# Attention and a gated feed-forward block on one core: when the loads of batch 2 and of the later queries are issued, a new planned order, and who turns tile 4

## The chip, the cores and the metric

One core of a Trainium2 chip. The time is the device time of one launch in microseconds (us). The engines are named as the profile names them: PE is TensorE (PEld its weight loads), DVE is VectorE, ACT is ScalarE, POOL is GpSimd, SP is the sync engine, which here only issues DMAs.

## The reference

```python
def _attn_ref(q, k, v):                     # 8 batches, 8 heads, 576 positions, 64 wide
    theta = np.pi / 2.0 * pos / S
    def phi(x, c, s):
        r = np.maximum(x, 0.0)
        return np.concatenate([r * c, r * s], axis=-1)
    q_p, k_p = phi(q, cos_w, sin_w), phi(k, cos_w, sin_w)
    kv = np.einsum('bhsf,bhsd->bhfd', k_p, v)
    z = np.sum(k_p, axis=2)
    num = np.einsum('bhsf,bhfd->bhsd', q_p, kv)
    den = np.einsum('bhsf,bhf->bhs', q_p, z)[..., None] + 1e-06
    return num / den

def _moe_ref(x, w_gate, w_val, w_out):      # x: 4608 tokens x 512; 1536 hidden
    g = x @ w_gate
    silu = g * (1.0 / (1.0 + np.exp(-g)))
    return silu * (x @ w_val) @ w_out
```

All inputs and the output are float32 in memory; the kernel casts its loads to 16 bits on the way in.

## The kernel before, in words

**Tiles and groups.** The 4608 tokens are 36 tiles of 128 rows (a batch is four and a half of them), and four tiles make one of nine groups (`tg` 0 to 8). For each batch `b` the kernel loads keys, values and queries (`load`, `load_turned`, on POOL's DMA queue: a key or value load is one instruction, a query load two), weighs them (relu on ACT, `vmul` on DVE), multiplies keys by values on PE (`kv_job`, the line L706), and turns the weighed queries by one long DMA on SP's queue (`phit<-r_q`, L905). For each tile `tile_jobs` (L823) then multiplies the turned queries with the key-value product, divides, and leaves a 128x512 tile `x`. The next stage needs that tile transposed (`xT`): `turn_job` does it by a DMA on SP's queue (L737), or, where its argument `by_pe` is true, by four transposes on PE and a copy on ACT (L745 and L597).

**The feed-forward part.** Group 0 and group 1 are computed plainly (L430, L928): gate and value products of 128x512 tiles. From group 2 on, gates are computed with a seven-product scheme (`block_jobs`, L999: each product is four matmuls of 256 columns), which first needs sums and differences of the turned tiles (`x_sum_jobs`, L972 on DVE, out of all four tiles of the group). The set `VAL` says for which groups the value products use that scheme as well, from `VAL_FROM` on; elsewhere `plain_val` computes them plainly. The scheme's summed weights are made once on DVE, by `weight_sums`. `out_jobs` (L1162) is the last product of a group, and `store_jobs` writes its rows.

**What sets the order.** From line 570 on nothing is issued at once: every piece is a `Job` with a duration for each engine that may do it and a list of jobs that it comes after, and `order_once` lays all of them out by a list schedule: at each step, for the engine that is free first, the most urgent ready job. What comes out is the program's order on each engine, fixed before the run; on the chip each instruction waits for its inputs. The planner starts its clock where the hand-written first part (`words`) ends; the first planned matmul of the profile stands at 27.5 us. `LOADED` gives the landing times of the loads of that first part, on the planner's clock. A DMA of the plan is put behind one running mark:

```python
            if j.dma:
                moved[0] = max(t + j.dma[0], moved[0]) + j.dma[1]
                j.done = moved[0] + LATER
```

with (1900, 600) ns for an `xT` transposition, (2500, 3300) for a load, and `LATER` 1500; due times count `X_LAND` 5200 for `xT`. `SEEDS` shake the urgencies, one number for each 10 us of PE's plan.

**Loads that are held.** `batch_loads` puts a tiny POOL copy (`hold_job`, L859) ahead of some loads, which reads a tile that must have landed first, so that the loads start only then. Everything behind that copy on POOL's queue, the stores among it, waits with it. Before the change: batch 2's keys and values wait for `xT` of tile 4; batch 3's queries for batch 2's turned queries; 3's keys and values for `xT` of tile 10; 4's queries, keys and values for 3's turned queries; 5's queries for `xT` of tile 15; 5's keys and values and 6's queries for 4's turned queries; 6's keys and values and 7's queries for 5's; 7's keys and values for 6's.

Of the kernel before, what the change touches and what calls it, by code (L numbers as in the profile page):

```python
# [19 lines left out]
def kernel(  # L20
# [584 lines left out]
    def relu_on(eng, out, in_):  # L605
# [7 lines left out]
    S_POOL = (1, 2, 4)  # L613
    S_GROUPS = ()
    LOADED = {("k", 1): 0.0, ("v0", 1): 6910.0, ("v1", 1): 8410.0, ("q0", 0): 2840.0, ("q0", 1): 10600.0, ("q1", 1): 18800.0,
              ("q", 2): 21600.0}
    WO_AT = ((0, 2, 11850.0), (2, 4, 13100.0), (4, 8, 15600.0), (8, 12, 18100.0))
    W_AT = {8: (1080.0, 2390.0), 10: (4150.0, 5460.0)}

    wg4 = wg_sb.rearrange("p (k c) (u w x) -> p w k c u x", k=2, w=2, x=P)  # L620
    wv4 = wv_sb.rearrange("p (k c) (u w x) -> p w k c u x", k=2, w=2, x=P)
# [112 lines left out]
    def turn_job(t, x, after, by_pe=False, key=None):  # L734
        if not by_pe:
            def fn(j):
                nc.sync.dma_start_transpose(out=xT_of(t), in_=one(x_all, x))  # L737
            J_["xT", t] = Job({"SP": 1450}, fn, after=after + J_.get(("xT_read", t // OUT - 3), []), put=[x], tail=X_LAND, dma=(1900.0, 600.0))
            return
        r = Room("bank")  # L740

        def fn(j):
            ps = bank(r).bitcast(FP16).rearrange("p (k x) -> p k x", x=P)
            for kc in range(KC):
                nc.tensor.transpose(out=ps[:, kc], in_=one(x_all, x)[:, kc * P:(kc + 1) * P], identity=ident16)  # L745
        mm = pe(230, fn, key, after=after, get=[r], put=[x])

        def fn(j):
            copied(j.eng, xT_of(t), bank(r).bitcast(FP16).rearrange("p (k x) -> p k x", x=P)[:, 0:KC])
        J_["xT", t] = Job({"ACT": sc(512)}, fn, after=[mm], put=[r])  # L750

    X_LAND = 5200.0
    PHI_LAND = 11500.0

    def half_tile_jobs(t, key, after, by_pe=False):
# [96 lines left out]
    def load_job(b, nm, after, lands, behind):  # L852
        def fn(j):
            (load_turned if nm == "q" else load)(b, nm)
        J_["load", b, nm] = Job({"POOL": 1600 if nm == "q" else 780}, fn, after=after, tail=lands, behind=behind, dma=(2500.0, 3300.0))

    def hold_job(read, after):
        def fn(j):
# [3 lines left out]
        return jb  # L862

    def batch_jobs(b, key):
        loaded_q = [J_["load", b, "q"]] if b > 2 else []
        landed = 0.0 if loaded_q else LOADED["q", 2]
        phis = []
        before = J_.get(("turned", b - 1), []) if b > 2 else J_["qt1"]

        def home():  # L870
            if (b, "q") not in st:
                st[b, "q"] = rel.tile([P, G, NC, 2, D], BF16, name="r_q")
            return st[b, "q"]
        if b in PHI_ACT:
            for c in range(NC):
                for w in range(2):
                    def fn(j, c=c, w=w):
                        nc.scalar.activation(out=home()[:, :, c, w], in_=raws[b, "q"][:, :, c], func=AF.Relu,
                                             scale=tanq[:, c:c + 1] if w else 1.0)
                    phis.append(Job({"ACT": 412}, fn, after=loaded_q + before + J_["tanq"], rel=landed))  # L880
        elif b in PHI_SWAP:
            for g in range(0, G, 2):
                def fn(j, g=g):
                    relu_on(j.eng, home()[:, g:g + 2, :, 0], raws[b, "q"][:, g:g + 2])
                phis.append(Job({"DVE": d4(1152)}, fn, after=loaded_q + before, rel=landed))
            for c in range(NC):
                def fn(j, c=c):
                    nc.scalar.activation(out=home()[:, :, c, 1], in_=raws[b, "q"][:, :, c], func=AF.Relu,  # L888
                                         scale=tanq[:, c:c + 1])
                phis.append(Job({"ACT": 430}, fn, after=loaded_q + before + J_["tanq"], rel=landed))  # L890
            J_["q_read", b] = list(phis)
        else:
            for g in range(G):
                def fn(j, g=g):
                    relu_on(j.eng, home()[:, g, :, 0], raws[b, "q"][:, g])
                re_ = Job(RELU_Q, fn, after=loaded_q + before, rel=landed)
                J_.setdefault(("q_read", b), []).append(re_)

                def fn(j, g=g):
                    tt(out=home()[:, g, :, 1], in0=home()[:, g, :, 0], in1=tabq2, op=ALU.mult)  # L900
                phis += [re_, Job({"DVE": d2(576)}, fn, after=[re_] + J_["tabq"])]
        J_["phi", b] = phis
        def fn(j):
            phit[b] = phip.tile([P, G, NC, SH, 2], BF16, name="phit")
            nc.sync.dma_start_transpose(out=phit[b].rearrange("p g c s e -> p (g c) (s e)"),  # L905
                                        in_=st[b, "q"].rearrange("p g c w d -> p (g c w d)"))
        turned = [Job({"SP": 7500}, fn, after=phis + J_.get(("tiles", b - 2), []), tail=PHI_LAND - 7500, dma=(2800.0, 6400.0))]
        J_["turned", b] = turned
        done = []
        for g in range(G):  # L910
            def fn(j, g=g):
                relu_on(j.eng, raws[b, "k"][:, g], raws[b, "k"][:, g])
            done.append(Job(RELU_K, fn, after=[J_["load", b, "k"]]))
            done.append(weight_job(b, g, [J_["load", b, "v"]] + ([J_["kvmm", b - 1]] if b > 2 else [])))
        J_["weighed", b] = done
        kv_job(b, key, done)

# [420 lines left out]
    for jj in range(J):  # L1338
        mm, o = turn_q_jobs(1, jj, 0, CUT, (0, 12.0 / 16), [rs[jj]])
        qa.append(o)  # L1340
        qmm.append(mm)
    plain_out_jobs((0, 0.76, 0.015))
    HALF_AT = (12.2, 12.6, 13.2, 13.8)
    for t, s, p in zip(range(4, 8), HALF_AT, (0, 1, 1, 1)):
        half_tile_jobs(t, (0, s / 16), lambda jj: [qa[jj]] + J_["qt0"] + J_["kv", 1], bool(p))
    for jj in range(J):
        mm, o = turn_q_jobs(1, jj, CUT, NC, (0, 15.5 / 16), [rs2])
# [41 lines left out]
    P2_AT = 3  # L1389
    P3_AT = {**{k_: 1.0 for k_ in range(1, 7)}, 7: 3.1}  # L1390
    GATE = set(range(2, NTG))
    VAL_FROM = 2
    VAL = {(tg, u) for tg in range(VAL_FROM, NTG) for u in range(3)}

    PLAIN = "g1 g3p v0 g7 g6 v2 g2 v1 g5 v3 g4".split()
    LAST = "v1 g3p v7 v6 v2 - v5 v4 - v3".split()
# [28 lines left out]

    APART = range(9, B)
    LAND = (6500.0, 7500.0, 8500.0)
    batch_loads(lambda: xT[1][0:1, 0, 0, 0:2], [J_["xT", 4]], [(2, "k"), (2, "v")])
    batch_jobs(2, (1, KV_AT[2] / 4))
    for tg in range(1, NTG):  # L1430
        b = tg + 2
        tiles = list(zip(range(max(9, 4 * tg + 4), 4 * tg + 8), TILES.get(tg + 1, ())))
        if 2 < b < B:
            def phit_read(b=b):
                return phit[b - 1][0:1, 0, 0, 0]
            names = {3: [(3, "q")], 4: [(4, "q"), (4, "k"), (4, "v")], 5: [(5, "k"), (5, "v"), (6, "q")],
                     6: [(6, "k"), (6, "v"), (7, "q")], 7: [(7, "k"), (7, "v")]}[b]
            batch_loads(phit_read, J_["turned", b - 1], names)
        for t, s in tiles:
            tile_jobs(t, (tg, s / 4))  # L1440
            if t == 10:
                batch_loads(lambda: xT[2][0:1, 2, 0, 0:2], [J_["xT", 10]], [(3, "k"), (3, "v")])
            if t == 15:
                batch_loads(lambda: xT[3][0:1, 3, 0, 0:2], [J_["xT", 15]], [(5, "q")])
        if b < B:
            batch_jobs(b, (tg + 1, KV_AT[b] / 4))
        if tg not in GATE:
            for fc in range(FC):
                plain_fc(tg, fc, (tg, fc / 4))
        else:  # L1450
            x_sum_jobs(tg)
            if ("wsum", "G") not in J_:
                weight_sums("G", wg4, {n: [J_["kvmm", 1]] for n in (2, 3, 4)}, list(gate_reads))
            if ("wsum", "V") not in J_ and (tg, 0) in VAL:
                weight_sums("V", wv4, {2: [J_["kvmm", 1]], 3: J_["num_done"], 4: J_["num_done"]}, list(val_reads))
            for u in range(3):
                at = places(tg, u)
                rooms, silus = silu_jobs(tg, u, block_jobs(tg, u, "G", gate_order(tg, u)))
                if (tg, u) in VAL:
                    order = [at[f"v{n}"] for n in (1, 7, 6, 2, 5, 4, 3)]  # L1460
                    block_mul_jobs(tg, u, rooms, silus, block_jobs(tg, u, "V", order))
                else:
                    for n, (i, w) in enumerate(((0, 0), (0, 1), (1, 0), (1, 1))):
                        plain_val(tg, u, i, w, rooms, silus, at[f"v{n}"])
# [24 lines left out]
    def order_once(nominal, seeds):  # L1489
# [31 lines left out]
            j.start = j.done = j.eng = None  # L1521
        free = {k: [(0.0, n) for n in range(n_)] for k, n_ in SIZE.items()}
        free["bank"] = [(t, n) for t, n in zip(BANK_AT, sorted(range(8), key=lambda x: used[x]))]
        is_filled, moved = [False] * 8, [LOADED["q", 2]]
        users = {}
        missing = {j: len(j.after) + len(j.behind) for j in jobs}
        est0 = {}
# [120 lines left out]
        return max(j.done for j in jobs if "PE" in j.engs)  # L1648

    RESERVE = 1  # L1650
    LATER = 1500.0
    SEEDS = (13881, 22536, 22536, 22536, 0, 12166, 85132, 39172, 44287, 22698, 22698, 53394, 50335, 50335, 92939, 92939, 92939, 0, 83505, 94269, 84613, 0, 0, 25880, 25880, 20639, 0)
    SHAKE = 1500.0
    WINDOW = 10000.0
    PACK = True
# [40 lines left out]
```

## Time and profile before

| | |
|---|---|
| median of three runs | 307.04 us (305.6; 307.04; and one of 1069.84) |
| the profiled execution's own time | 309.23 us |
| its span, first to last instruction | 307.4 us |
| mean granted clock of PE | 0.986 |
| PE busy | 295.6 us, 96% |
| DVE, ACT, POOL busy | 249.9, 201.0 and 70.3 us |
| read from memory, written to it | 37.75 MB, 9.44 MB |

The profiled execution took 2.19 us more than the median, and 1.83 us of its time lie outside the span. The page shows each engine's busy share in 40 slices of 7.7 us; below it stand the DMA engines' share and the clock that PE was granted. The other views used here are the waits by engine, the chain of work that ended last, the timeline of one engine, busy times by stretches, and the DMA issues of a stretch with the time to their landing.

### The profile page before, as it was taken

To read this page: it belongs to the slowest core of one execution; us is meant where nothing else is said; L and a number is where in the kernel's file an instruction comes from. 1 tells how busy PE (TensorE), PEld (TensorE's weight loads), DVE (VectorE), ACT (ScalarE), POOL (GpSimd) and SP (SyncE) were. 2 spreads that over 40 slices of the span, in tenths; PEclk is the share of its full clock that TensorE was granted. 3 is DMA by queue.
4 is the path that set the end of the run, shared out by engine and by line. 5 is a ranking of instruction groups with operands and counts; after the bars stand their busy time and mean duration, and the time that the engine had idled before them with its cause. 6 is when DMAs were issued, how large, how long until landed. Compare 5 with 4: busy or idle time off the path is not lost.

```text
span 307.4 us, 7913 instructions
## 1 busy us (share of the span) xinstructions
PE 295.6 (96%) x3170; PEld 237.2 (77%) x3170; DVE 249.9 (81%) x507; ACT 201.0 (65%) x427; POOL 70.3 (23%) x126
## 2 busy tenths in 40 slices
PE   8999999999999999995999999999999999999991
PEld 4597455455887988883888889888888988888880
DVE  7766769999978998893798994999779959967971
ACT  8564448954897795993589659986475556636430
POOL 7754402010208021800323202200220050002020
PEclk9999999999999999997899999999999999999998
DMA  7999999997899999999499792670262153002026
GB/s 259 225 197 197 205 204 140 224 147 125 125 203 186 193 161 151 141 187 232 60 211 186 156 171 71 120 145 13 57 109 46 19 124 67 0 2 68 2 70 138
DMA packets 72357, 41.02 MB, mean 133 GB/s; under 512 B 49280, under 2 KB 69248, under 8 KB 72320
## 3 DMA queue, kind: packets, MB, share of 16 engines
q0 software_dynamic: 24992, 24.91, 49.2%
q1 hardware_dynamic: 46880, 15.21, 27.4%
q10 hardware_dynamic: 448, 0.39, 0.6%
q8 instruction: 25, 0.41, 0.5%
q14 instruction: 12, 0.10, 0.1%
HBM read 37.75 MB, written 9.44 MB: 153 GB/s over the span
## 4 chain that ended last, share of the span: by engine, by line
PE 87%; DMA 7%; ACT 1%; DVE 1%; SPq 1%; issue 1%; DVEq 0%; ACTq 0%
PE banks L999 39%; PE banks L1162 24%; PE banks L928 10%; DMA xT<-x 4%; PE banks L430 3%; PE banks L1271 3%; PE banks L706 3%; DMA ht<-in_k_dram 2%; PE banks L823 2%; SPq L151 1%; PE banks L364 1%; PE banks L766 1%; ACT sg L1058 1%; PE banks L1305 0%; ACT banks L597 0%
## 5 line engine op out<-in xcount | busy, mean ns | idle before, releaser
L1131 POOL DMA_DIRECT2D out_dram<-ob x56 | 29.6, 537 | 125.0 <-ACT ob L599 91.6
L1092 DVE TENSOR_TENSOR ht<-sg,banks 128x512 f16<-128x512 bf16 x63 | 42.3, 682 | 3.2 <-PE banks L999 3.1
L1162 PEld LDWEIGHTS <-ht 128*128 128x128 f16 x384 | 37.8, 98 | 5.4 <-issue 0.5
L1058 ACT ACTIVATE sg<-banks 128x512 bf16<-128x512 f32 x63 | 35.8, 597 | 7.2 <-PE banks L999 5.9
L597 ACT COPY banks<-banks 128x512 f32<-128x512 f32 (+1 forms) x51 | 29.4, 581 | 15.4 <-PE banks L1162 9.4
L999 PEld LDWEIGHTS <-wgs_sb 128*128 128x128 f16 x336 | 32.7, 99 | 8.5 <-DVE kvt L972 3.6
L1019 DVE TENSOR_TENSOR banks<-m,banks 128x512 f32<-128x512 f32 x42 | 28.9, 692 | 9.1 <-PE banks L999 6.2
L999 PEld LDWEIGHTS <-wg_sb 128*128 128x128 f16 x336 | 32.6, 98 | 4.0
L999 PE MATMUL banks<-kvt,wgs_sb 128*128 128x256 f16 x216 | 32.3, 278 | 3.5 <-DVE kvt L972 3.4
L999 PEld LDWEIGHTS <-wv_sb 128*128 128x128 f16 x336 | 32.3, 98 | 4.3 <-issue 0.2
L599 ACT ACTIVATE ob<-banks 128x512 f32<-128x512 f32 x34 | 20.0, 597 | 23.6 <-PE banks L1162 18.7
L1162 PEld LDWEIGHTS <-sums 128*128 128x128 f16 x288 | 28.2, 99 | 3.6
L597 ACT COPY m<-banks 128x512 f32<-128x512 f32 x42 | 24.4, 588 | 8.1 <-PE banks L999 8.1
L1162 PE MATMUL banks<-wo_sb,ht 128*128 128x256 f16 x192 | 26.3, 276 | 0.2 <-ACT banks L597 0.2
L999 PE MATMUL banks<-xT,wg_sb 128*128 128x256 f16 x168 | 25.7, 276 | 0.0
L1162 PE MATMUL banks<-wt_sb,sums 128*128 128x256 f16 x192 | 25.4, 279 | 0.0
L999 PE MATMUL banks<-xT,wv_sb 128*128 128x256 f16 x168 | 24.8, 273 | 0.0
L1162 PE MATMUL banks<-wt_sb,ht 128*128 128x256 f16 x192 | 22.4, 272 | 0.0
L1058 ACT ACTIVATE sg<-m 128x512 bf16<-128x512 f32 x21 | 13.2, 631 | 10.8 <-DVE m L1027 10.7
L269 DVE TENSOR_TENSOR v<-raw_kv,tab 128x1152 bf16<-128x1152 bf16 x27 | 19.3, 754 | 0.4 <-ACT raw_kv L451 0.4
L888 ACT ACTIVATE r_q<-raw_q,tanq 128x256 bf16<-128x256 bf16 x45 | 19.6, 502 | 0.0
L999 PE MATMUL banks<-kvt,wv_sb 128*128 128x256 f16 x144 | 19.5, 273 | 0.0
(153 smaller groups left out, 566.6 us busy)
## 6 DMA issues: line engine op xcount, KB each, us to landing
out_dram<-ob POOLq DMA_DIRECT2D x56, 128.0 KB, 2.9
raw_kv<-in_k_dram POOLq DMA_DIRECT2D x7, 576.0 KB, 7.7
raw_q<-in_q_dram POOLq DMA_DIRECT2D x12, 288.0 KB, 8.3
raw_kv<-in_v_dram POOLq DMA_DIRECT2D x6, 576.0 KB, 9.3
out_dram<-ob SPq DMA_DIRECT2D x12, 128.0 KB, 2.6
wg_sb<-in_moe_w_gate_dram POOLq DMA_DIRECT2D x5, 256.0 KB, 9.1
wv_sb<-in_moe_w_val_dram POOLq DMA_DIRECT2D x5, 256.0 KB, 9.5
wo_sb<-in_v_dram SPq DMA_DIRECT2D x2, 576.0 KB, 4.1
```

The source lines that it names most:

```text
L269: nc.vector.tensor_tensor(out=v2s[b == 1][:, g, :, :, 0:D], in0=(first if b == 0 and g == 0 else {"v": raw_of(b, "v")})["v"][:, g].unsquee ...
L430: nc.tensor.matmul(out=st["f", tg, fc, lo][i], lhsT=(wg_sb, wv_sb)[i][:, kc, fs], rhs=xT[tg][:, ts, kc], start=(kc == 0), stop=(kc == KC - 1))
L597: nc.scalar.copy(out=out, in_=in_)
L599: nc.scalar.mul(out=out, in_=in_, mul=mul)
L888: nc.scalar.activation(out=home()[:, :, c, 1], in_=raws[b, "q"][:, :, c], func=AF.Relu, scale=tanq[:, c:c + 1])
L928: nc.tensor.matmul(out=bank(r), lhsT=w[:, kc, fc * P:(fc + 1) * P], rhs=xT[tg][:, :, kc], start=(kc == 0), stop=(kc == KC - 1))
L999: nc.tensor.matmul(out=to[:, i], lhsT=a[:, c, 2 * u + i], rhs=x()[:, :, c], start=first and i == 0 and c == 0, stop=c == KH - 1, skip_grou ...
L1019: tt(out=bank(c), in0=one(m7_all, m).rearrange("p i x -> p (i x)"), in1=bank(b), op=ALU.add)
L1058: nc.scalar.activation(out=gates(rooms[w])[:, :, jh * HT:(jh + 1) * HT], in_=src, func=AF.Silu, scale=DOWN)
L1092: tt(out=ht[:, 4 * u + w:4 * u + w + 3:2, jh * HT:(jh + 1) * HT], in0=gates(rooms[w])[:, :, jh * HT:(jh + 1) * HT], in1=src.rearrange("p ( ...
L1131: {"POOL": nc.gpsimd, "SP": nc.sync, "ACT": nc.scalar}[j.eng].dma_start(out=out_v[idx // NC, idx % NC][:, cols], in_=ob_of(t)[e * SH:(e + ...
L1162: nc.tensor.matmul(out=to, lhsT=a[:, kc, i * P:(i + 1) * P], rhs=b[:, kc], start=first and kc == 0 and i == 0, stop=kc == HC - 1, skip_gro ...
```

## The change

Seven things, all in the planned part or just ahead of it:

- the keys and values of batch 2 are loaded right behind the first part's loads, with no hold;
- batch 4's queries are loaded behind batch 3's values (under the hold on `xT` of tile 10), batch 6's behind a new hold on `xT` of tile 19, batch 7's behind a new hold on `xT` of tile 23; they leave their places under the holds on turned queries;
- tile 4 is turned by PE and ACT, not by DMA;
- the value products of group 2 are computed plainly (`VAL_FROM` 3), and the value weights' sums come with group 3;
- the planner counts longer DMAs: 1000 ns for an `xT`, 3500 for a load, `LATER` 2200, `X_LAND` 7000;
- its running mark starts at the latest landing of the first part;
- other `SEEDS`, and so another order of the planned work.

```diff
     LOADED = {("k", 1): 0.0, ("v0", 1): 6910.0, ...
-              ("q", 2): 21600.0}
+              ("k", 2): 24900.0, ("v", 2): 28200.0, ("q", 2): 21600.0}
...
+    load(2, "k")
+    load(2, "v")
...
-            J_["xT", t] = Job({"SP": 1450}, fn, ..., tail=X_LAND, dma=(1900.0, 600.0))
+            J_["xT", t] = Job({"SP": 1450}, fn, ..., tail=X_LAND, dma=(1900.0, X_SVC))
...
-    X_LAND = 5200.0
+    X_LAND = 7000.0
+    X_SVC = 1000.0
...
-        J_["load", b, nm] = Job({"POOL": 1600 if nm == "q" else 780}, fn, ..., dma=(2500.0, 3300.0))
+        J_["load", b, nm] = Job({"POOL": 1600 if nm == "q" else 780}, fn, ..., dma=(2500.0, 3500.0))
...
-            done.append(Job(RELU_K, fn, after=[J_["load", b, "k"]]))
-            done.append(weight_job(b, g, [J_["load", b, "v"]] + ([J_["kvmm", b - 1]] if b > 2 else [])))
+            done.append(Job(RELU_K, fn, after=loaded("k"), rel=landed_at("k")))
+            done.append(weight_job(b, g, loaded("v") + ([J_["kvmm", b - 1]] if b > 2 else []), landed_at("v")))
...
+    BY_PE = (1, 1, 1, 1)
-    for t, s, p in zip(range(4, 8), HALF_AT, (0, 1, 1, 1)):
+    for t, s, p in zip(range(4, 8), HALF_AT, BY_PE):
...
-    VAL_FROM = 2
-    VAL = {(tg, u) for tg in range(VAL_FROM, NTG) for u in range(3)}
+    VAL_FROM = 3
+    VAL_MORE = set()
+    VAL = {(tg, u) for tg in range(VAL_FROM, NTG) for u in range(3)} | VAL_MORE
...
-    batch_loads(lambda: xT[1][0:1, 0, 0, 0:2], [J_["xT", 4]], [(2, "k"), (2, "v")])
...
-            names = {3: [(3, "q")], 4: [(4, "q"), (4, "k"), (4, "v")], 5: [(5, "k"), (5, "v"), (6, "q")],
-                     6: [(6, "k"), (6, "v"), (7, "q")], 7: [(7, "k"), (7, "v")]}[b]
+            names = {3: [(3, "q")], 4: [(4, "k"), (4, "v")], 5: [(5, "k"), (5, "v")], 6: [(6, "k"), (6, "v")],
+                     7: [(7, "k"), (7, "v")]}[b]
...
             if t == 10:
-                batch_loads(lambda: xT[2][0:1, 2, 0, 0:2], [J_["xT", 10]], [(3, "k"), (3, "v")])
+                batch_loads(lambda: xT[2][0:1, 2, 0, 0:2], [J_["xT", 10]], [(3, "k"), (3, "v"), (4, "q")])
             if t == 15:
                 batch_loads(lambda: xT[3][0:1, 3, 0, 0:2], [J_["xT", 15]], [(5, "q")])
+            if t in (19, 23):
+                batch_loads(lambda t=t: xT[t // 4][0:1, 3, 0, 0:2], [J_["xT", t]], [(t // 4 + 2, "q")])
...
-        is_filled, moved = [False] * 8, [LOADED["q", 2]]
+        is_filled, moved = [False] * 8, [max(LOADED.values())]
...
-    LATER = 1500.0
-    SEEDS = (13881, 22536, 22536, 22536, 0, 12166, ...)
+    LATER = 2200.0
+    SEEDS = (75955, 75955, 42606, 56809, 39745, 39745, ...)
```

More of the change, by code (lines that the diff above doesn't have):

```diff
@@ L737, in fn @@
                 nc.sync.dma_start_transpose(out=xT_of(t), in_=one(x_all, x))
-            J_["xT", t] = Job({"SP": 1450}, fn, after=after + J_.get(("xT_read", t // OUT - 3), []), put=[x], tail=X_LAND, dma=(1900.0, 600.0))
+            J_["xT", t] = Job({"SP": 1450}, fn, after=after + J_.get(("xT_read", t // OUT - 3), []), put=[x], tail=X_LAND, dma=(1900.0, X_SVC))
             return
@@ L854, in fn @@
             (load_turned if nm == "q" else load)(b, nm)
-        J_["load", b, nm] = Job({"POOL": 1600 if nm == "q" else 780}, fn, after=after, tail=lands, behind=behind, dma=(2500.0, 3300.0))
+        J_["load", b, nm] = Job({"POOL": 1600 if nm == "q" else 780}, fn, after=after, tail=lands, behind=behind, dma=(2500.0, 3500.0))
     def hold_job(read, after):
@@ L864, in batch_jobs, with loaded, landed_at @@
     def batch_jobs(b, key):
-        loaded_q = [J_["load", b, "q"]] if b > 2 else []
+        def loaded(nm):
+            return [J_["load", b, nm]] if b > 2 else []
+        def landed_at(nm):
+            return 0.0 if b > 2 else LOADED[nm, 2]
+        loaded_q = loaded("q")
         landed = 0.0 if loaded_q else LOADED["q", 2]
@@ L1453 @@
                 weight_sums("G", wg4, {n: [J_["kvmm", 1]] for n in (2, 3, 4)}, list(gate_reads))
-            if ("wsum", "V") not in J_ and (tg, 0) in VAL:
+            if ("wsum", "V") not in J_ and any((tg, u) in VAL for u in range(3)):
                 weight_sums("V", wv4, {2: [J_["kvmm", 1]], 3: J_["num_done"], 4: J_["num_done"]}, list(val_reads))
@@ L1650 @@
     RESERVE = 1
-    LATER = 1500.0
-    SEEDS = (13881, 22536, 22536, 22536, 0, 12166, 85132, 39172, 44287, 22698, 22698, 53394, 50335, 50335, 92939, 92939, 92939, 0, 83505, 94269, 84613, 0, 0, 25880, 25880, 20639, 0)
+    LATER = 2200.0
+    SEEDS = (75955, 75955, 42606, 56809, 39745, 39745, 31519, 31519, 3815, 87805, 83741, 46593, 46593, 3103, 71530, 57274, 57274, 57274, 61673, 61673, 22451, 0, 0, 27447, 57540, 26502, 0)
     SHAKE = 1500.0
```

## The prediction, made before the changed kernel was run

> **What bounds the kernel now.** I read the page first, its rows of busy tenths:
>
> ```profile
> span 307.4 us, 7913 instructions
> ...
> PE   8999999999999999995999999999999999999991
> DVE  7766769999978998893798994999779959967971
> ACT  8564448954897795993589659986475556636430
> ...
> PEclk9999999999999999997899999999999999999998
> DMA  7999999997899999999499792670262153002026
> ```
>
> PE is busy in every slice but one: slice 19, around 146 us, shows 5, and the granted clock falls to 7 and 8 in slices 19 and 20. Nothing else can shorten the run but less PE work or that hole. Second, PE's waits, which say whether there is another hole:
>
> ```profile
> PE banks L999 <- DVE kvt L972: 3.4, 1, 3.4
> PE banks L188 <- DVE zeros L183: 1.0, 1, 1.0
> PE banks L928 <- ACT xT L597: 0.2, 1, 0.2
> ```
>
> There is not: one wait of 3.4 us on the group's sums (L972), one at the very start, and some of 0.1 to 0.2 us, about 0.7 us in all. Third, the chain that ended last, at that place (start, length, what):
>
> ```profile
> 129.31 12.89 DMA xT<-x
> 142.24 0.04 issue
> 142.29 0.44 DVE kvt L972
> ```
>
> The sums waited for the last transposed tile of group 4 (tile 19), issued at 129.31 us and landed 12.89 us later. Fourth, the DMA issues of two stretches (KB each, us to landing): first 120.2 to 130 us, then 180 us to the end.
>
> ```profile
> out_dram<-ob POOLq DMA_DIRECT2D x8, 128.0 KB, 6.2
> raw_kv<-in_k_dram POOLq DMA_DIRECT2D x1, 576.0 KB, 9.6
> raw_kv<-in_v_dram POOLq DMA_DIRECT2D x1, 576.0 KB, 12.4
> raw_q<-in_q_dram POOLq DMA_DIRECT2D x2, 288.0 KB, 13.9
> xT<-x SPq DMA_TRANSPOSE x4, 10.6
> ```
>
> ```profile
> xT<-x SPq DMA_TRANSPOSE x12, 3.3
> ```
>
> The same transposition takes 3.3 us with the DMA engines free and 10.6 us beside a batch of keys, values, queries and stores. The planner had counted on 1.9 + 0.6 + 1.5 = 4.0 us. Last, the busy times by stretches (us, PE, PEld, DVE, ACT, POOL, then PE's clock, DMA share, GB/s):
>
> ```profile
> 140.00:144.00 4.00, 1.23 (x6) 0.89 (x7) 1.71 (x5) 0.16 (x1) 0.00 (x0) 0.75 1.25 219
> 144.00:148.00 4.00, 4.00 (x21) 2.87 (x19) 1.59 (x3) 2.17 (x4) 0.00 (x0) 0.50 1.06 180
> 148.00:152.00 4.00, 4.00 (x41) 3.45 (x40) 3.38 (x9) 2.37 (x6) 2.21 (x4) 0.90 0.14 7
> ```
>
> After the hole PE runs at half clock until about 148.7 us. The loss: half of the 1.23 us busy in the first row (0.6), 4 x 0.5 = 2.0, and 4 x 0.1 = 0.4: 3.0 us. So the hole costs 3.4 + 3.0 = **6.4 us**.
>
> [...]
>
> **The change part by part.** The sum is made against the profiled execution, 309.23 us.
>
> *The queries' loads.* The burst behind the hole was keys and values of batch 5 (POOL, 124.46 and 127.34 us), two query loads of batch 6 (128.13 us, 1.31 us of issue) and eight stores. The change takes batch 6's queries out; they wait for tile 19 itself. It also takes batch 4's queries out of the burst at 97 us, beside which the tiles of group 3 took 8.8 to 11.8 us. They come behind batch 3's values, which landed at 87.5 us, so near 91 us and not 102.6 us; batch 4's turned queries, issued at 110.6 us and landed at 121.2 us, can come up to 10 us earlier, and the hold on them, at 121.3 us, and batch 5's loads with it. What remains late is the last tile of group 4, and it is late by less than the 3.4 us. Holds on POOL: one goes (tile 4), two come (tiles 19 and 23), each a copy of 0.2 to 0.8 us and two issues of 0.6 us. Behind them on POOL stand stores and the next hold, which waited 20 us at 149 us anyway; stores have two buffers. On the path: nothing. If that cover is gone, a store late by a hold delays ACT's eviction, which once waited 4.3 us for a store already. I count the whole hole as gone, **-6.4 us**; the bounds are 0 and -6.4.
>
> *Batch 2's keys and values.* The two issues (0.75 us each) move from 50.2 us to about 38 us, into a stretch where POOL waited 13 us at a hold. In the DMA queue they stand behind batch 2's queries, which landed at 49.1 us. Alone a load takes 3.1 us (57.85 to 60.92 us between the two landings), so they land near 52.2 and 55.3 us, 5.6 us earlier than before. Six stores of group 0, landed by 58.2 us, get later by up to 6 us; their buffers are next wanted at 63 us and later. The turned queries of batch 2 took 10.2 us from 56.2 us beside these loads and took 7.3 us alone (201 us), so they come 2 to 3 us earlier, and with them tiles 9 to 11. PE had no gap there: 0 on the path, up to 3 us of margin for group 2.
>
> *Tile 4.* Four transposes on PE, 0.22 us (L745 x4 at 48.77 us), and one ACT copy of 0.59 us, where ACT is at 5.6 of 10 busy: **+0.2 us**. At 53.6 us PE waited 0.23 us for the last such copy of group 1; one more copy ahead of it may add up to 0.6 us.
>
> *The plain value products of group 2.* A value block of four columns is 7 products of four matmuls; 20 of these took 2.18 us (L999 at 84.86 us), so 28 take 3.05 us. Plain, four columns are 4 x 4 = 16 matmuls of 128x512 columns, and 16 of those took 3.45 us (L928 at 73.72 us). The difference is 0.40 us, three times a group: **+1.2 us**. DVE gets rid of two adds (0.69 + 0.68 us) and pays 0.26 us more in the products, ACT of two copies of 0.58 us, each three times: -3.3 us and -3.5 us, off the path. The value weights' sums (four of 0.96 us on DVE) move behind: DVE at 8.4 to 9.5 of 10 busy there has room for them as long as they come before group 3's first value product. If not, PE waits up to 3.8 us.
>
> *The planner's numbers and the order.* Each planned transposition now lands 0.4 + 0.7 = 1.1 us later than it was counted, and more behind other DMAs, so tiles are made earlier ahead of their group. Groups 7 and 8 had their last tile at 234.23 and 257.24 us and their sums at 234.33 and 257.26 us: no margin, yet no wait of PE. No row shows the new order. It can win back at most the 0.7 us of small gaps; the other end is a new hole, bounded by the one of before, 6.4 us. I take 0, because the old order had one hole in nine groups and the new one is laid with more room.
>
> Sum: 309.23 - 6.4 + 0.2 + 1.2 = 304.2 us on the profiled execution, which stood 2.19 us above the median of 307.04. If that is the cost of profiling, the forecast is 302.1 us; if the hole was merely wider in that execution, it is 304.3 us without it. I take the middle, **303.2 us**, 1.3% less than before, with 301 to 306 as its own range.
>
> **Rivals.** *A, the hole gets narrower only.* Tile 19 landed at 142.20 us, between batch 5's values (139.76) and the second half of batch 6's queries (143.15). So it didn't stand behind the queries as a whole; they only shared the engines with it for the last 2.4 us. If half of these are won, 1.2 us, a wait of 2.2 us is left: 303.2 + 2.2 = 305.4 us, or 308.4 us with the half clock. Against it: batch 5's loads come earlier as a whole. [...]
>
> *B, a new hole at group 2 (slower).* Batch 4's queries now make a third load of the burst that the hold on tile 10 lets go at 78 us. Tile 11 was issued at 76.31 us, 1.9 us ahead of the burst, and landed at 78.78 us, 1.5 us before the sums. If the new order issues it, or a tile of a later group, after a burst of three, it takes 10.6 to 12.9 us and not 3.3: 7.3 to 9.6 us late, less 1.5 us of margin, plus 3.0 us at half clock: +8.8 to +11.1 us. The last tile of a burst paid the most (tile 19, 12.9 us), so I take the upper end, 303.2 + 11.1 = 314.3 us; the lower is 312. It decides from about 2 us between the issues of tiles 10 and 11. For it: four of the seven groups from 2 on (3, 4, 7 and 8) had margins under 0.5 us. Against: 2 us is more than tiles 10 and 11 were apart (74.37 and 76.31), and the planner knows of the loads.
>
> *C, the profile costs more than the median says.* Against the lowest run, 305.6, the offset is 3.63 us, and the forecast is 304.2 - 3.6 = 300.6 us, 2.1% faster. Against it: PE does 1.4 us more work.
>
> **How the numbers follow.** Forecast 0.50, A 0.17, B 0.20, C 0.13. About 2% is what a measurement of this kernel can tell from no change: below 300.9 us is faster, above 313.2 us slower. C gives faster 0.13, forecast and A same 0.67, B slower 0.20. The range of 300.4 to 313.5 us leaves out a third of C (0.04) and some two thirds of B (0.13).
>
> **What would show it.** Right: no wait of PE above 1 us after the start, a clock of 1.00 in all stretches between 20 and 300 us, group 4's tiles landing before their sums, three transposed tiles by PE become four, group 2's value products on L1068 to L1080, keys of batch 2 landing by 53 us. Wrong: a PE wait on L972 or L928 of over 2 us with a half clock behind it, at whatever group (A at group 4, B at group 2); or PE busy throughout and still over 306 us, which would mean that the plain products cost more than 1.2 us.

## The result, and the profile after

The changed kernel takes 302.02 us (median of four runs, 301.84 to 302.41) beside 306.75 us for the kernel before (median of four runs, one of them of 1069.84): a ratio of 0.986, 95% interval 0.983 to 0.989. Ratios, here and below, leave out executions more than 1.5% above the fastest of their kernel. Within 2% of no change, as forecast, and 1.2 us below the predicted 303.2 us. Its profiled execution took 301.84 us.

The page after: span, then busy tenths by slice (now 7.5 us each).

```profile
span 300.0 us, 7830 instructions
...
PE   8999999999999999999999999999999999999992
...
PEclk9999999999999999999999999999999999999999
```

PE has no hole left, and the clock records show full clock from 4.1 to 297.6 us. PE's waits:

```profile
PE banks L188 <- DVE zeros L183: 1.0, 1, 1.0
PE banks L936 <- ACT xT L597: 0.6, 1, 0.6
PE banks L339 <- DVE wgs_sb L331: 0.4, 1, 0.4
```

The wait on the group's sums is gone; the longest one after the start is 0.6 us, for the fourth copy of a tile turned by PE (0.23 us before). The DMA issues of 117 to 130 us, in which group 4's tiles are turned (KB each, us to landing):

```profile
out_dram<-ob POOLq DMA_DIRECT2D x8, 128.0 KB, 6.1
raw_kv<-in_k_dram POOLq DMA_DIRECT2D x1, 576.0 KB, 6.5
raw_kv<-in_v_dram POOLq DMA_DIRECT2D x1, 576.0 KB, 9.0
xT<-x SPq DMA_TRANSPOSE x4, 7.1
```

The queries are out of this burst, the other loads land 3 us sooner after their issue, and the transpositions take 7.1 us in place of 10.6. Tile 19 is issued at 128.8 us and lands at 136.4 (before: 129.3 and 142.2); the sums start at 141.0 us, 4.6 us later. The same stretches as before, by engine (us, PE, PEld, DVE, ACT, POOL, PE's clock, DMA share, GB/s):

```profile
140.00:144.00 4.00, 4.00 (x39) 3.57 (x37) 4.00 (x9) 3.12 (x7) 0.00 (x0) 1.00 1.12 153
144.00:148.00 4.00, 4.00 (x39) 3.58 (x38) 4.00 (x9) 2.04 (x4) 0.00 (x0) 1.00 0.99 172
```

PE's last matmul ends at 294.43 us in place of 300.84, 6.4 us earlier, and the stores behind it end 5.6 us later in place of 6.6.

### The profile page after: what moved, and what is told of

Read it like the earlier page. It is cut to its first block, busy times and chain, and to the rows that moved or that the text cites. A ratio compares the mean times of both kernels' runs of the same rounds, so it can differ in the third digit from the quotient of the medians.

```text
span 300.0 us, 7830 instructions
## 1 busy us (share of the span) xinstructions
PE 292.2 (97%) x3138; PEld 232.6 (78%) x3138; DVE 247.3 (82%) x502; ACT 198.8 (66%) x421; POOL 71.5 (24%) x127
## 4 chain that ended last, share of the span: by engine, by line
PE 92%; DMA 2%; DVE 2%; ACT 1%; SPq 1%; issue 1%
PE banks L1007 40%; PE banks L1170 25%; PE banks L936 9%; PE banks L430 4%; PE banks L1082 3%; PE banks L1279 3%; PE banks L826 2%; DMA ht<-in_k_dram 2%; PE banks L708 2%; SPq L151 1%; PE banks L769 1%; PE banks L364 1%; DVE wgs_sb L269 0%; DVE ht L954 0%; ACT raw_kv L257 0%
## 5 line engine op out<-in xcount | busy, mean ns | idle before, releaser
L1100 DVE TENSOR_TENSOR ht<-sg,banks 128x512 f16<-128x512 bf16 x54 | 36.4, 681 | 3.8 <-PE banks L1007 3.6
L597 ACT COPY banks<-banks 128x512 f32<-128x512 f32 (+1 forms) x48 | 27.3, 578 | 13.4 <-PE banks L1170 6.2
L1007 PEld LDWEIGHTS <-wgs_sb 128*128 128x128 f16 x324 | 31.5, 98 | 4.7
L1027 DVE TENSOR_TENSOR banks<-m,banks 128x512 f32<-128x512 f32 x39 | 27.0, 692 | 7.3 <-ACT m L597 4.6
L1007 PEld LDWEIGHTS <-wv_sb 128*128 128x128 f16 x288 | 27.8, 98 | 3.4
L1007 PE MATMUL banks<-kvt,wgs_sb 128*128 128x256 f16 x204 | 29.2, 273 | 0.0
L597 ACT COPY m<-banks 128x512 f32<-128x512 f32 x39 | 22.7, 589 | 5.8 <-PE banks L1007 5.5
L1007 PE MATMUL banks<-xT,wv_sb 128*128 128x256 f16 x144 | 21.5, 273 | 0.0
L1007 PE MATMUL banks<-kvt,wg_sb 128*128 128x256 f16 x144 | 19.8, 273 | 0.0
L848 DVE TENSOR_TENSOR x<-banks,rec 128x512 f16<-128x512 f32 x27 | 18.5, 688 | 1.4
## 6 DMA issues: line engine op xcount, KB each, us to landing
raw_q<-in_q_dram POOLq DMA_DIRECT2D x12, 288.0 KB, 10.2
```

Source lines behind the costliest of these rows:

```text
L597: nc.scalar.copy(out=out, in_=in_)
L848: tt(out=one(x_all, x).rearrange("p (y e d) -> p e y d", e=2, d=D), in0=view()[:, :, :, 0:D], in1=rec_all[:, t % 4].rearrange("p (e y) o - ...
L1007: nc.tensor.matmul(out=to[:, i], lhsT=a[:, c, 2 * u + i], rhs=x()[:, :, c], start=first and i == 0 and c == 0, stop=c == KH - 1, skip_grou ...
L1027: tt(out=bank(c), in0=one(m7_all, m).rearrange("p i x -> p (i x)"), in1=bank(b), op=ALU.add)
L1100: tt(out=ht[:, 4 * u + w:4 * u + w + 3:2, jh * HT:(jh + 1) * HT], in0=gates(rooms[w])[:, :, jh * HT:(jh + 1) * HT], in1=src.rearrange("p ( ...
```

## The experiments

Two theories of why the hole went. **L**: batch 6's queries no longer share the DMA engines with group 4's last tiles. **O**: the new order makes the tiles earlier or wants them later, and the loads matter little. In e1, e2 and e5 the list of planned jobs is left as it is and only the named DMAs and their holds change places in it; in e6 a DMA stands in the place of four transposes and a copy. So every engine's order, and the buffers that the plan gave to each tile, stay those of the parent. (The ratios are to the kernel before.)

**e1: the order of before, batch 6's queries held behind tile 19.**

```diff
...
+    order = sorted(jobs, key=lambda j: j.start)
+    late = J_["load", 6, "q"]
+    order.remove(late)
+    held = hold_job(lambda: xT[4][0:1, 3, 0, 0:2], [])
+    at = order.index(J_["xT", 19]) + 1
+    order[at:at] = [held, late]
...
```

> The order of the kernel before on every engine, with one thing moved: batch 6's query loads wait behind tile 19's transposition (as in the changed kernel) and no longer follow batch 5's values. Theory L (the hole went because those loads no longer share the DMA engines with group 4's last tiles): tile 19 lands 2.5 us or more earlier than 142.2, the wait of PE falls from 3.4 us to under 1 us, no half clock, 301 to 302.5 us. Theory O (the new order made the room; the loads matter little): tile 19 lands at 141 us or so, a wait of about 2.2 us is left, 304 to 306 us.

Measured: 303.99 us, ratio 0.9895 (0.982 to 0.997). Chain (start, length) and PE's wait:

```profile
129.61 10.72 DMA xT<-x
```

```profile
PE banks L999 <- DVE kvt L972: 1.2, 1, 1.2
```

Tile 19 lands 1.9 us earlier (140.3 us), and the wait falls from 3.4 to 1.2 us. No half clock follows it; the granted clock is 0.995 to 0.998 in all four executions. Beside the profiled execution of the kernel before, these loads alone are thus worth 2.2 us of wait and the 3 us of half clock, and leave 1.2 us to the order, which lies between the two theories. Part of the 3 us belongs to that one execution: three of the seven executions of the kernel before in the same comparison also had 0.995 or 0.996, and took 305.2 to 306.0 us.

**e2: the order of the changed kernel, batch 6's queries back behind batch 5's values.**

```diff
+    soon = J_["load", 6, "q"]
+    order.remove(soon)
+    order.insert(order.index(J_["load", 5, "v"]) + 1, soon)
...
```

> The changed kernel's order on every engine, with batch 6's query loads put back right behind batch 5's values. Theory L: tile 19 lands 3 to 5 us later than 136.4 us, the margin of 4.6 us before the sums is eaten, a wait of 0.5 to 2 us appears, 302.5 to 305 us. Theory O: the sums stand late enough in the new order, no wait of PE, 302.0 us within 0.3.

Measured: 302.3 us, ratio 0.983 (0.978 to 0.989). The queries' row in the DMA issues of 117 to 131 us, then all of PE's waits:

```profile
raw_q<-in_q_dram POOLq DMA_DIRECT2D x2, 288.0 KB, 12.6
```

```profile
PE banks L188 <- DVE zeros L183: 1.0, 1, 1.0
PE banks L936 <- ACT xT L597: 0.6, 1, 0.6
```

With the burst back, tile 19 lands at 140.0 us, 3.6 us later, as theory L priced it; the sums, at 141.46 us, are still behind it, and PE does not wait. In the new order the moved queries are a reserve that this place does not use. What removes the wait here is the rest of the change together, the new order with the other moved loads in it: the sums start 2.7 us behind the place where DVE was ready for them before (141.46 and 138.72 us), and the tile lands 2.2 us earlier. e2 does not part the one from the other.

**e8: the changed kernel with the seeds' shake off.**

```diff
-    SEEDS = (75955, 75955, 42606, 56809, ...)
+    SEEDS = (0,)
```

> The changed kernel with the planner's shake off (one seed, zero), so that only the order of the planned work differs. Theory S (the order found by the seeds carries much of the time, and the four other parts are worth little by themselves): many small waits of PE on DVE and ACT, 308 us or more. Theory L/O (places of the loads and room for the DMAs carry it): no wait behind a transposition, 302 to 304 us.

Measured: 309.96 us, ratio 1.011 (1.004 to 1.018). That is theory S's time: with all other parts of the change in place, but in a plan made without the search, the kernel is slower than before. The planner itself ends PE's work 10.2 us later in this plan (277.6 us on its clock) than in that of the changed kernel (267.4). No run has the kernel before without its seeds, so what the other parts are worth in such a plan is not shown. No long wait: eleven kinds, 5.4 us in all beside the start's 1.0, the longest 0.9.

**e4 and e11: the planner's longer numbers alone, in the kernel before.** e4 keeps its seeds; for e11 they were searched anew, for the earliest end of PE in the plan.

```diff
-    X_LAND = 5200.0
+    X_LAND = 7000.0
-            ... dma=(1900.0, 600.0))
+            ... dma=(1900.0, 1000.0))
-        ... dma=(2500.0, 3300.0))
+        ... dma=(2500.0, 3500.0))
-    LATER = 1500.0
+    LATER = 2200.0
```

> The kernel before with the planner's longer DMA numbers alone (1000 and 3500 ns, 2200, 7000), old seeds, old places of the loads, tile 4 by DMA, group 2's value products by the scheme. Theory O: the longer numbers alone make room for the tiles, no wait over 1 us on PE, 300 to 302 us (1.4 us less PE work than the changed kernel). Theory L: the burst at 124 us is as dense as before, group 4's sums still wait 2 to 4 us, 304 to 308 us.

> The kernel before with the planner's longer DMA numbers alone, and seeds searched anew for them. Theory O (room in the order is enough, wherever the loads stand): no wait behind a transposition, and the time is below 305 us. Theory L (with the loads in bursts the order can make that room only by running DVE and ACT dry elsewhere): no such wait either, but small waits of PE on DVE and ACT add up to 3 us or more, 305 to 308 us.

Measured: e4 312.23 us, ratio 1.016 (1.010 to 1.022); e11 309.55 us, ratio 1.010 (1.007 to 1.014). In e4 no transposition is waited for by PE; the time goes in small waits, of which the largest sums are these.

```profile
PE banks L1162 <- DVE banks L1205: 2.4, 3, 1.1
PE banks L999 <- DVE banks L1019: 1.2, 3, 0.5
```

In e11 there is a long one again, at another place. PE's wait, and DVE's timeline there (start, length, what, and last the idle time before with its releaser):

```profile
PE banks L999 <- DVE x L845: 3.5, 1, 3.5
```

```profile
161.31 1.29 DVE L845 TENSOR_TENSOR x<-banks,rec 128x512 f16<-128x512 f32 x2 [3.39 <-DMA xT<-x]
```

DVE has tile 22 of `x` to write, and the plan has put it into the buffer of tile 20, which a transposition still reads (issued at 151.8 us, landed at 161.2). The plan had counted on 5.1 us for that transposition; it took 9.4. Two of the four buffers were free, those of tiles 18 and 19, whose transpositions had landed by 142.1 us. A late transposition thus stops PE without any sum being due. Both theories missed: there was a long wait, which O excluded and L did not expect either. In these two plans the longer numbers, with the loads in their old places, bring nothing. Both plans were longer from the start: PE's work ends at 282.5 us (e4) and 270.4 us (e11) on the planner's clock, in the kernel before at 267.3. That fits L's reason, room for the transpositions at the cost of work elsewhere; whether a longer search would find a better plan is open.

**e9 and e12: the changed kernel in two other good orders.** Both have seeds searched anew; e9 also has the planner's old DMA numbers.

```diff
 e9 and e12:
-    SEEDS = (75955, 75955, 42606, 56809, ...)
+    SEEDS = (...)
 e9 alone:
-    X_LAND = 7000.0
-    X_SVC = 1000.0
+    X_LAND = 5200.0
+    X_SVC = 600.0
-    LATER = 2200.0
+    LATER = 1500.0
-        ... dma=(2500.0, 3500.0))
+        ... dma=(2500.0, 3300.0))
```

> The changed kernel (loads spread, tile 4 by PE, plain value products in group 2) with the planner's old DMA numbers (600 and 3300 ns, 1500, 5200) and seeds searched anew for them. If the longer numbers are what keeps the tiles ahead of their sums, tiles land after the sums' place again at one group or more: PE waits of 1 to 3 us on a transposition, 303.5 to 307 us. If spreading the loads is enough, no wait over 0.6 us: 301.5 to 302.5 us.

> The changed kernel with other seeds, searched anew with all its numbers and places kept: a second good order, as a control for e9 (which had a second good order and the planner's old DMA numbers). If the longer numbers are what makes an order hold on the chip, this one has no wait of PE above 0.6 us and takes 301.5 to 302.7 us. If the recorded order was simply a lucky one, waits of 1 us or more appear here too, 303 to 306 us.

Measured: e9 303.27 us, ratio 0.991 (0.987 to 0.995), its executions from 302.25 to 306.83; e12 303.12 us, ratio 0.987 (0.984 to 0.990). In e9 the margin is gone at group 5: tile 23 lands at 177.5 us, the sums start at 177.6 after 2.2 us of waiting, and PE waits:

```profile
PE banks L1007 <- DVE kvt L980: 1.4, 2, 1.1
```

So in this plan, made with the shorter numbers, a transposition comes late. That the numbers are the cause, or that they cost time, is not shown: e12, with the longer ones, has nearly the same median, and in the two plans PE's work ends within 0.1 us of each other (267.3 and 267.4 us on the planner's clock). What the execution of 306.83 us waited for no trace tells. In e12 four executions took 302.7 to 303.2 us, and two 308.2 and 308.7; its profile is of one of those two (PE's wait, then ACT's timeline):

```profile
PE banks L826 <- ACT ob L599: 2.1, 1, 2.1
```

```profile
184.10 0.42 ACT L886 ACTIVATE r_q<-raw_q 128x256 bf16<-128x256 bf16 x1 [4.64 <-DMA phit<-r_q]
184.55 0.60 ACT L599 ACTIVATE ob<-banks 128x512 f32<-128x512 f32 x1
```

Batch 7's queries, loaded behind tile 23 now, run beside the turning of batch 6's queries; ACT may not overwrite the one `r_q` buffer until that DMA has read it, waits 4.6 us, and the evictions behind it on ACT keep PE waiting. No other execution of e12 has a trace, so that the four shorter ones lack this wait is not shown; their granted clock was 0.994 to 0.999, that of the two long ones 0.986. In the changed kernel that DMA became longer too (14.5 us from 162.3 us, before 8.8 us), but there the first relu that overwrites the buffer starts 2.6 us behind its landing (179.4 and 176.8 us). So the moved loads have a cost of their own, and the recorded order is one in which it is covered. The control e12 answers to neither expectation alone: four of its executions lie at or just above the first range, two above the second.

**e5: batch 2's keys and values held behind tile 4 again, the order of the changed kernel.**

```diff
-    load(2, "k")
-    load(2, "v")
...
+    held = hold_job(lambda: xT[1][0:1, 0, 0, 0:2], [])
+    loads = Job({"POOL": 1560}, lambda j: (load(2, "k"), load(2, "v")))
+    at = order.index(J_["xT", 4]) + 1
+    order[at:at] = [held, loads]
...
```

> The changed kernel's order on every engine, with batch 2's keys and values loaded behind a hold on tile 4 again, as before. My prediction counted their early place at nothing on the path: then no wait of PE appears, 302.0 us within 0.5. Rival: the new order is built on the early landing (51.7 and 55.8 us; batch 2's key-value products stand at 61.9 us on PE). Held, the values land near 60 us and need four products of 0.75 us on DVE, so PE waits 2 to 3 us at those products: 304 to 307 us.

Measured: 307.6 us, ratio 1.004 (1.001 to 1.007). That is 0.6 us above the rival's range, and the wait is at another place: PE waits at group 1's start. PE's wait, and ACT's timeline there:

```profile
PE banks L934 <- ACT xT L597: 4.2, 1, 4.2
```

```profile
56.58 0.68 ACT L257 ACTIVATE raw_kv<-raw_kv 128x576 bf16<-128x576 bf16 x1 [3.56 <-DMA raw_kv<-in_k_dram]
...
58.36 0.56 ACT L597 COPY xT<-banks 128x512 f16<-128x512 f16 x1
```

In this order a relu of batch 2's keys stands on ACT ahead of the copy of group 1's last tile. With the keys landing at 56.6 us and not at 51.7, it holds the copy up, and 3.4 us of half clock follow (the granted clock of that execution was 0.992).

**e6: tile 4 turned by DMA, the order of the changed kernel.**

```diff
             ps = bank(r).bitcast(FP16)...
+            if t == 4:
+                nc.sync.dma_start_transpose(out=xT_of(t), in_=one(x_all, x))
+                return
...
+            if t == 4:
+                return
             copied(j.eng, xT_of(t), ...
```

> The changed kernel's order, with tile 4 turned by a DMA on SP's queue instead of four transposes on PE and a copy on ACT. If the turn by PE only costs its 0.2 us: 301.8 us, the transposition lands by 52 us (it took 4.4 us before the change). Rival: beside batch 2's keys and values, which fill the DMA engines until 55.8 us, it takes 8 us or more and group 1's first matmul (54.8 us) waits 1 to 3 us: 303 to 305 us.

Measured: 305.78 us, ratio 0.9985 (0.995 to 1.002), 0.8 us above the rival's range. The transposition takes 8.1 us (45.7 to 53.8) beside batch 2's loads, as the rival said; but it is not group 1's matmul that waits for it. PE's wait, and DVE's timeline there:

```profile
PE banks L750 <- DVE x L810: 2.4, 1, 2.4
```

```profile
53.89 0.76 DVE L810 TENSOR_TENSOR x<-numtmp,rec 128x256 f16<-128x256 f32 x2 [3.32 <-DMA xT<-x]
```

It is the `x` buffer again. The plan of the changed kernel puts tile 6 into the buffer of tile 4, which the turn by PE frees early, and uses two of the four buffers for tiles 4 to 7; now DVE waits until the DMA has read tile 4. The turn by PE, four transposes of 0.2 us in all, is worth 3.8 us in a plan that was made for it. With another buffer for tile 6 this wait would not arise, and the transposition (landed at 53.8 us) would be in time for group 1's first product (54.8 us); no run has that.

**e7 and e10: the value products of group 2 by the seven-product scheme** (e7 with the changed kernel's seeds, e10 with seeds searched anew).

```diff
-    VAL_FROM = 3
+    VAL_FROM = 2
```

> The changed kernel with the value products of group 2 by the seven-product scheme again (planned anew with the same seeds). If the plain products cost only PE work, as in my sum: 1.2 us less, 300.8 us, and no wait over 0.5 us. Rival: the plain products bought room on DVE (3.3 us) and ACT (3.5 us) between 80 and 115 us; then DVE's queue delays tiles or sums of group 3, PE waits 1 us or more there, 302 to 305 us.

> The changed kernel with the value products of group 2 by the seven-product scheme, and seeds searched anew for that, so that the order is not the cause that e7 may have had. If the plain products only cost PE work: 301 us. If they bought room on DVE and ACT (3.3 and 3.5 us, and four weight sums of 0.96 us that come later): 304 to 307 us, with waits of PE on DVE and ACT between 80 and 125 us.

Measured: e7 310.71 us, ratio 1.011 (1.005 to 1.017); e10 306.74 us, ratio 1.003 (0.999 to 1.007). The first lies above both of its ranges and mostly shows an order made for other work. The second is the fair one: 1.2 us less PE work, and yet 4.7 us more. PE's busy time in it, by stretches of 40 us (second column):

```profile
20.00:60.00 40.00, 39.03 (x322) 22.91 (x320) 29.15 (x72) 25.53 (x56) 9.97 (x14) 1.00 1.19 195
...
100.00:140.00 40.00, 38.56 (x449) 33.19 (x448) 34.55 (x70) 32.44 (x73) 8.18 (x17) 1.00 1.03 159
```

It is idle for 1.0 us in the first and 1.4 us in the second of these, and for 0.4 us in each of the two other stretches up to 180 us, on ACT's evictions and copies and on DVE's tiles. That fits the rival (the plain products bought room on DVE and ACT), and so does the plan: with 1.2 us less PE work to lay, PE's work ends at 271.1 us on the planner's clock, in the changed kernel at 267.4. Whether a longer search would find a shorter plan is open.

## Why the prediction was right

The sum was 309.23 - 6.4 + 0.2 + 1.2 = 304.2 us for the profiled execution; that of the changed kernel took 301.84 us, 2.4 us less. Term by term, from the starts of PE's matmuls in the two traces:

| step | predicted, us | measured, us |
|---|---|---|
| the hole and its half clock | -6.4 | -6.4 (3.5 idle, 28 matmuls 0.104 late each) |
| tile 4's turn on PE | +0.2 | +0.2 |
| plain value products | +1.2 | +1.2 (48 matmuls, 10.37, in place of 84, 9.18) |
| small waits, order | 0, at best -0.7 | -1.4 |
| behind PE's last matmul | not counted | -1.0 |

The first three steps came out as priced. The **hole** went as a whole, and rival A, which left 2.2 us of it, is what e1 shows for the moved queries alone (1.2 us left); the forecast held because the order added the rest, a part that I had counted at nothing. The place of batch 6's queries, the first reason given for the 6.4 us, is not what the final kernel lives on: with them put back it takes 302.3 us and does not wait (e2). So the size of this step held, and its reason only in part. One link failed: batch 4's turned queries, forecast up to 10 us earlier, landed 1.4 us later (122.6 us in place of 121.2), and batch 5's keys, whose hold they release, were issued only 1.2 us earlier (123.3 us in place of 124.5).

The **order** is the mis-sized term: 2.4 us, beyond the bound of 0.7 us. That bound took only the gaps that PE's waits list, and these stayed as they were. The gain lies in matmuls that start later than the median spacing of their shape: between 90 and 130 us they did so by 3.7 us in all before, and by 2.3 us after; between 20 and 90 us the new order loses 0.6 us, and behind 130 us, the hole apart, it wins as much. The end was left out: PE's last matmul was followed by 6.6 us of stores with the old order (before, e1) and by 5.6 us with the new one (after, e2). e8, with all parts but the searched order, is some 8 us slower than the changed kernel, and no step of the prediction had a term for that. The premise that nothing but less PE work or the hole could shorten the run was thus wrong by these 2.4 us.

The **offset** between the profiled execution and the median was put down half to profiling. It was none: the profiled execution of the changed kernel lies 0.2 us below its median. The 2.19 us go with the half clock of that one execution, whose granted clock was 0.986. Of 58 later executions of the kernel before, 31 had a granted clock of 0.993 or more and took 304.1 to 307.1 us; 25 had 0.989 to 0.992 and took 306.3 to 309.4 us; two had 0.986 and took 309.3 and 310.5 us. So in about half of its executions the hole seems to bring no half clock, and the 6.4 us are the dear end: between the medians the change won 4.7 us, between the two profiled executions 7.4. The other executions have no trace, so how long their waits were is not shown. The middle that I took, 1.0 us below the sum, made up for 1.0 of the 2.4 us by luck.

**Batch 2's loads and tile 4.** "0 on the path" was right for the change as a whole, and no more: e5 and e6 show that the new order, as it was planned, needs both, at 5.6 and 3.8 us. The cover that I named for the tile, ACT's room, was not the point; the buffer of `x` that its early turn frees was.

**Plain products.** Priced as a cost of 1.2 us, with 3.3 us on DVE and 3.5 us on ACT off the path. e10 makes it likely that they pay for themselves, which the prediction did not say.

**Rival B** did not occur at group 2: tiles 10 and 11 are issued at 71.8 and 75.1 us, ahead of the burst at 76.5. Its mechanism, a moved query load beside something that is waited for, is what e12 met at batch 6's turned queries. **Rival C** had 300.6 us, from an offset that does not exist.

## What to carry to other kernels

When one wait in a trace names a transfer, look at what shares the engines with it and at when its result is wanted: e1 removed most of it by the one (3.4 us became 1.2), e2 all of it by the other (with other loads moved as well). In a schedule fixed before the run, a part is worth what it is worth in that order; judge it in the same order (by moving its instructions alone), and then with a new one. A late transfer also stopped the writer of the buffer that it still read (DVE for 3.39 us in e11 and 3.32 us in e6, ACT for 4.64 us in e12), so look at which buffer the plan hands to whom; moving instructions alone keeps that choice, and part of what such a run measures can be its price (e6).

## What was not expected of the hardware

**The half clock behind a wait of PE did not follow the wait's length.** By the clock records it lasted 6.83 us in the kernel before (after a wait of 3.4 us) and 6.8 us in e12 (waits of 2.1 us and shortly behind it 0.8 us), 3.4 us in e5 (after 4.2 us) and in e6 (after 2.4 us). In e11, after 3.52 us of idle from 158.5 to 162.05 us, there was none, and none after 1.2 us in e1 (granted clock 0.998). Stretches of e6, of e12 and of e11 (us, PE, PEld, DVE, ACT, POOL, clock, DMA share, GB/s):

```profile
52.00:54.00 2.00, 0.00 (x0) 0.00 (x0) 0.11 (x1) 0.00 (x0) 0.00 (x0) 1.00 1.19 222
54.00:58.00 4.00, 3.63 (x15) 1.76 (x16) 3.31 (x11) 1.89 (x4) 0.00 (x0) 0.57 0.61 195
```

```profile
184.00:188.00 4.00, 1.99 (x15) 1.46 (x15) 1.81 (x4) 3.87 (x12) 1.65 (x3) 0.65 0.48 50
188.00:192.00 4.00, 4.00 (x27) 2.94 (x26) 2.79 (x7) 2.76 (x9) 2.12 (x4) 0.50 1.23 195
```

```profile
156.00:160.00 4.00, 2.53 (x41) 1.87 (x38) 0.74 (x3) 3.84 (x10) 3.17 (x6) 1.00 1.29 158
160.00:164.00 4.00, 1.95 (x18) 1.76 (x19) 1.89 (x3) 0.95 (x3) 1.05 (x2) 1.00 1.16 300
```

The length in e6 is worked out from its second line (4 us at 0.57: 4 x 0.43 / 0.5 = 3.4 us), that in e12 from its two lines in the same way (2.8 and 4.0 us). So a wait of 2.4 us had 3.4 us of half clock behind it, and one of 3.5 us had none. What decides between the two is not shown by these runs.
